# A sliding-window attention block with an MLP on one core: loads six blocks ahead, q and k turned four blocks ahead, and the start and the decay tables rearranged

## The chip, the core and the metric

The kernel runs on one core of a Trainium2 chip. The metric is the device time of one execution in microseconds (us). A core has a matrix engine (PE; its weight loads are listed as PEld), a vector engine (DVE), an activation engine (ACT), GpSimd (POOL) and SyncE (SP). Each engine works through its own list of instructions in order. In this kernel POOL and SP mostly issue DMA transfers, each from its own queue.

## The reference

Inputs are q, k, v of shape (8 batches, 8 heads, 576 tokens, 64), a norm gain g_ln (512), and weights w_ch1 (512 x 2048) and w_ch2 (2048 x 512), all in f32.

```python
scores = q @ k.T / sqrt(64)                      # per batch and head
rel = pos[:, None] - pos[None, :]
scores = scores - slope[h] * abs(rel)            # slope[h] = 2 ** -(h + 1)
attn = softmax(where((rel >= 0) & (rel < 128), scores, -1e9))
x = (attn @ v), heads side by side               # (8, 576, 512)
xn = (x - mean(x)) / sqrt(var(x) + 1e-6) * g_ln
out = x + maximum(xn @ w_ch1, 0) @ w_ch2
```

## The kernel before

**Blocks.** The eight batches are taken as four pairs. A pair has nine blocks of 128 tokens: blocks 0 to 7 alternate between its two batches (four each), and block 8 holds the last 64 tokens of both. So there are 36 blocks, numbered n = 0 to 35 in the list order; n = 9p + blk. One load or turn of q or k serves two blocks (one per batch).

**A block's way.** POOL loads q, k (L225, L228) and v (L238) with casts to f16 into raw buffers. q and k are then turned (transposed), so that the head dimension lies on partitions. PE makes the scores (scores, L446; products L423) for the block's own and the preceding 128 tokens. ACT takes the exponential (L432). DVE multiplies with a mask (masks, L443) that holds the window and the decay exp(-slope x distance). PE multiplies with v (L478), DVE divides by the row sums (L486, L487) to give x, and centres or normalizes it (xc, L517 or L553). xc is turned to xT, and the block is then ready for the MLP. On most blocks POOL computes rstd (L534, L537) ahead of xc.

**Two ways of turning.** For the blocks of the first pair, PE turns q, k and xc and ACT or DVE copies them out of PSUM (L295, L324, L325, L574, L575). From the second pair on (`by_dma`), SP turns them with DMA transpositions: q of the one batch, q of the other, k of the one, k of the other (L313), and xT (L529). These wait on SP's queue in list order, and so do the stores of the output (L926, L930).

**The MLP.** Blocks are grouped: six groups of two, then six of four. mlp1 multiplies xT with w1 in units of four products (L734); ACT or DVE applies the relu into ht (L750, L742). Four PSUM buffers (ps_mm) take the units in turn. mlp2 multiplies with w2 (L767); from group 6 on, `fast_mlp2` (L804, L833) does that with seven instead of eight block products. DVE adds x (L851), and SP stores.

**Decay tables.** The masks are exp(-slope x distance), made by `decay` (L118) on ACT, one instruction a head, from the constant `dist` (128 x 896, f16): m_full, used by the first pair; m_ends and m_tail, for the last block of a pair; m_late, for all later pairs.

**What sets the order.** The order is written out by hand: `steps` is a list of steps, each a list of calls. `weave_at(units, places)` hands out the MLP's units and runs a step at each given place, so that every engine's list follows from the order of calls. Up to block 7 the steps are written one by one. From block 8 on a loop makes them: for each n, the value products of n, the scores of n + 2, the statistics and xc of n with the loads for a later block (`load_step`, L629, which issues all of `place` up to it), the masks, and the turns (`turn_at`, L681). Loads run `AHEAD` = 8 blocks ahead. In the loop the turns of q and k by DMA are called with n + 1 and take block n + 5. They read what the loads brought, and the scores of their block read them.

These lines of before stand in the loop:

```python
stats_step = [(stats, n)] + load_step(n)
turns = [turn_at(n + 1)] if n + 1 < count else []
...
steps += [stats_step + to_mask, [(normal, n)], *turns]
```

Of the kernel before, what the change touches and what calls it, by code (L numbers as in the profile page):

```python
# [17 lines left out]
P = 128  # L18
# [12 lines left out]
AHEAD = 8  # L31
# [28 lines left out]
def kernel(  # L60
# [39 lines left out]
    iden_dram = nc.inline_tensor(np.eye(P, dtype=np.float16), name="iden16")  # L100
    dist_dram = nc.inline_tensor(distances(), name="distances")
    dist = consts.tile([P, 7 * P], FP16)
    nc.sync.dma_start(out=dist, in_=dist_dram.ap())
    iden = consts.tile([P, P], FP16)
    ps_sc = [
        ps_scores.tile([P, 2, 4 * P], FP32, name=f"ps_sc{i}", tag=f"ps_sc{i}")
# [8 lines left out]
    m_full = hsum[0]  # L115
    m_tail = consts.tile([P, H, P], FP16)

    def decay(m, at):  # L118

        n = m.shape[2]  # L120
        for h in range(H):
            nc.scalar.activation(  # L122
                out=m[:, h, :],
                in_=dist[:, at * P : at * P + n],
                func=AF.Exp,
                scale=-(2.0 ** (-8.0 * (h + 1) / H)),
            )
# [50 lines left out]
    def combine_w2():  # L178


        for dst, a, b in (
# [5 lines left out]
            for part in range(2):  # L187
# [3 lines left out]
                )  # L191
                yield

    def load_w2(c):
        n = NFB // 4
        nc.gpsimd.dma_start(
            out=w2[:, c * n : (c + 1) * n, :], in_=w2r[:, c * n : (c + 1) * n, :]
        )
# [44 lines left out]

    order = [(p, blk) for p in range(NPAIR) for blk in range(NSLOT)]
    w1s, w2s = ([(f, c) for c in range(4)] for f in (load_w1, load_w2))
    weights = {3: w1s + w2s[:2], 5: w2s[2:]}
    loads, place = [], []
    for n, (p, blk) in enumerate(order):
        for src, tag in ((q, "q"), (k, "k")):
# [22 lines left out]
    def warm(n):  # L272

        if n:
            ps = ps_mm.tile([P, 4 * P], FP32, tag="mm", name="ps_warm")
        for _ in range(n):
            nc.tensor.matmul(ps, ones[:, 0:P], ones, start=True, stop=True)  # L277
# [113 lines left out]
    def attend(p, blk, keys, mask, tag, hps):  # L391

        heads = slice(2 * hps[0], 2 * hps[-1] + 2)
        nk = len(keys)
        if hps[0] == 0:
            home_pool = own_pool if tag == "own" else probs_pool  # L400
            pr = home_pool.tile([P, H, nk, P], FP16, tag=tag, name=tag)
            for t, o in enumerate(keys):
                weights_of.setdefault((p, blk), []).append((pr, t, o))
        else:
            pr = weights_of[p, blk][-1][0]
        at = len(scored) % 2
        banks = ps_sc[at]
        scored.append((p, blk))
        ps = banks.rearrange("p j (n t q) -> p j n t q", n=len(hps), t=nk)
        qt, b = turned["q", p, blk // 2], blk % 2  # L410
        for n, hp in enumerate(hps):
            for t, o in enumerate(keys):
                kt = turned["k", p, o // 2][:, o % 2]
                for j in range(2):
                    rows = slice(j * HALF, (j + 1) * HALF)
                    for c, queries in seen(p, blk, o, t, junk[at] and j == 0):
                        cols = slice(c * HALF, (c + 1) * HALF)
                        at_q, of_q = ps[cols, j, n, t, :], qt[rows, b, hp]
                        if len(of_q.shape) == 3:
                            at_q = at_q.rearrange("p (r c) -> p r c", r=2)  # L420
                        else:
                            at_q, of_q = at_q[:, queries], of_q[:, queries]
                        nc.tensor.matmul(  # L423
                            at_q,
                            kt[rows, hp, cols],
                            of_q,
                            start=True,
                            stop=True,
                        )
        junk[at] = False  # L430
        dst = pr[:, heads].rearrange("p h t q -> p h (t q)")
        nc.scalar.activation(  # L432
            out=dst.rearrange("p (n j) q -> p j n q", j=2),
            in_=ps.rearrange("p j n t q -> p j n (t q)"),
            func=AF.Exp,
            scale=inv_sqrt_d,
        )
        unmasked.setdefault((p, blk), []).append((dst, mask[:, heads, :]))
# [4 lines left out]
            nc.vector.tensor_tensor(out=dst, in0=dst, in1=mask, op=ALU.mult)  # L443
        del todo[:n]

    def scores(p, blk, between=0):  # L446
        low, high, every = [0, 1], [2, 3], [0, 1, 2, 3]
        m = m_late if by_dma(p, blk // 2) else m_full
        if blk == T:
            attend(p, T, [6, 7], m_ends, "probs", low)  # L450
            attend(p, T, [6, 7], m_ends, "probs", high)
        elif blk < 2:
            attend(p, blk, [blk], m[:, :, P:], "own", every)
        else:
            attend(p, blk, [blk - 2, blk], m, "probs", low)
            warm(between)
            attend(p, blk, [blk - 2, blk], m, "probs", high)

    def scores_tail(p):
        attend(p, T, [T], m_tail, "own", [0, 1, 2, 3])  # L460
# [164 lines left out]
        return [(scores,) + order[n]]  # L625

    def load_step(n):
        return [(load_until, place[min(n + AHEAD, count - 1)])]

    def values_steps(n):  # L630
        p, blk = order[n]
# [5 lines left out]
    def x_step(n, copy=nc.vector.tensor_copy):  # L637
        return [(turn_x,) + home[n] + order[n] + (copy,)] if n < BY_DMA else []
# [5 lines left out]
    def masks_of(n, *halves):  # L644
        return [(masks,) + order[n] + halves]
# [8 lines left out]
    steps += warm_step(2) + [turn_step(2, True, (nc.scalar.copy, nc.scalar.copy))]  # L654
    steps += values_steps(1) + warm_step(4)
    steps += [x_step(0, nc.scalar.copy)] + warm_step(2) + [scores_step(2)]
    steps += [masks_of(2, 1) + x_step(1) + [(warm, 2), (scores, 0, 3, 2)]]
    steps += [values_steps(2)[0]]
    steps += [masks_of(2)]
    first = len(steps)  # L660

    steps += [values_steps(2)[1] + masks_of(3)]
    steps += [x_step(2, nc.scalar.copy), *values_steps(3), x_step(3, nc.scalar.copy)]

    steps += [variance_of(0) + variance_of(1), variance_of(2) + variance_of(3)]
    steps += [[(gain_w1, 0, 13)]]

    steps += [turn_step(4, True) + [(gain_w1, 13, 3)], scores_step(4), masks_of(4) + values_steps(4)[0]]
    steps += [values_steps(4)[1], scores_step(5) + [(decay, m_ends, 2)]]
    steps += [x_step(4) + masks_of(5)]  # L670
    steps += [values_steps(5)[0], turn_step(6, True), values_steps(5)[1], scores_step(6)]
    steps += [x_step(5) + masks_of(6), scores_step(7) + variance_of(4), values_steps(6)[0]]

    steps += [values_steps(6)[1], x_step(6) + masks_of(7), variance_of(5) + [(decay, m_late, 5)]]
    steps += [*values_steps(7), x_step(7) + variance_of(6)]
    steps[-1] += turn_step(9)
    steps += [turn_step(8) + variance_of(7), scores_step(8) + turn_step(11)]
    steps += [[(scores_tail, 0)] + scores_step(9) + masks_of(8)]


    def turn_at(n):  # L681
        ahead = [m for m in (n + 3, n + 4) if m < count and order[m][1] % 2 == 0]
        return [
            f
            for m in ahead
            if by_dma(order[m][0], order[m][1] // 2) == (m == n + 4)
            for f in turn_step(m, True)
        ]

    steps.append([])  # L690
    for n in range(8, count):
        first_half, second_half = values_steps(n)
        step = first_half + second_half[:1]
        if n == BY_DMA + 2:
            step = [(turn_x,) + home[n - 1] + order[n - 1] + (nc.scalar.copy,)] + step
        if n + 1 < count and order[n + 1][1] == T:
            step += [(scores_tail, order[n][0])]
        if n + 2 < count:
            step += scores_step(n + 2)
        steps.append(step)  # L700
        to_mask = [m for t in (n + 1, n + 2) if t < count for m in masks_of(t)]
        stats_step = [(stats, n)] + load_step(n)
        turns = [turn_at(n + 1)] if n + 1 < count else []
        if n == HURRIED:
            steps += [[(normal, n - 1)], stats_step + to_mask, [(normal, n)], *turns]
        elif n >= SETTLED:
            steps += [stats_step + to_mask, [(normal, n)], *turns]
        else:
            steps += [stats_step + to_mask, *turns]
            if n != HURRIED - 1:  # L710
                steps.append([(normal, n)])
# [234 lines left out]
    nc.vector.memset(powers[:, 0:1], EPS)  # L946
    nc.vector.memset(powers[:, 1:2], -0.5)
    decay(m_full, 0)
    decay(m_tail, 4)
    load_until(place[3])  # L950
    engine = mybir.EngineType
    with tc.manual_schedule(engines={engine.PE, engine.SP, engine.Pool}):
        with tc.manual_schedule(engines={engine.Activation, engine.DVE}):
            advance_to(first)
            weave_at(mlp1(0, (0, 1)), 2, 7, 8, 9, 13)
            weave_at(mlp1(1), 2, 8, 12)
            weave_at(mlp2(0, ((0, 8), (8, 12), (12, NFB))), 0, 1, 3, 4, 4, 5)
            weave_at(mlp2(1), 0, 1, 2, 3, 4, 6, 6)
            weave_at(mlp1(2), 0, 3, 3, 6, 8, 11)
            weave_at(mlp2(2), 0, 2, 4, 6, 7)  # L960


            weave_at(mlp1(3, (9, 10, 11)), 8, 8, 12, 15)
            weave_at(mlp2(3), 0, 1, 1, 3, 4, 4, 6, 6)
            weave_at(mlp1(4), 0, 4, 8, 10, 10, 14, also=(2, 12))
            weave_at(mlp2(4), 0, 2, 2, 5, 5, 7, also=(1,))
            weave_at(mlp1(5), 0, 4, 4, 6, 8, 10, also=(3, 7, 11))
            weave_at(mlp2(5), 0, 1, 2, 4, 6, 7)
            ring += [ps_mm.tile([P, DM], FP32, tag="mm", name="ps_r") for _ in range(4)]
            for g in range(6, len(GROUPS)):  # L970
                weave_at(
                    mlp1(g), 0, 2, 5, 7, 8, 10, 13, 15, also=(1, 4) if g == 6 else ()
                )
                weave_at(fast_mlp2(g), 1, 3, 6, 7, 7, 10, 12, 13)
# [31 lines left out]
```

## Time and profile before

| | us |
|---|---|
| median of 3 runs | 309.25 (307.91 to 310.70) |
| the profiled execution | 309.62 |
| its span, first to last instruction | 307.8 |
| PE busy | 298.4 |
| DVE busy | 218.8 |
| ACT busy | 171.6 |
| POOL busy | 143.4 |

The profile is one execution; the span is 1.8 us shorter than that execution's own time, since something lies around the instructions. A row of instructions reads: line, engine, operation, output <- inputs, shape; then times. A wait is printed as "engine line <- what released it: us in total, times, longest us". In the chain that ended last, each row has its start, its duration and what it was. Transfers: issuing queue, operation, count, KB each, median us from issue to landing; a transposition shows no KB. The granted clock of PE was 0.992 of full speed as a mean over the span.

### The profile page before, as it was taken

To read this page: it belongs to the slowest core of one execution; us is meant where nothing else is said; L and a number is where in the kernel's file an instruction comes from. 1 tells how busy PE (TensorE), PEld (TensorE's weight loads), DVE (VectorE), ACT (ScalarE), POOL (GpSimd) and SP (SyncE) were. 2 spreads that over 40 slices of the span, in tenths; PEclk is the share of its full clock that TensorE was granted. 3 is DMA by queue.
4 is the path that set the end of the run, shared out by engine and by line. 5 is a ranking of instruction groups with operands and counts; after the bars stand their busy time and mean duration, and the time that the engine had idled before them with its cause. 6 is when DMAs were issued, how large, how long until landed. Compare 5 with 4: busy or idle time off the path is not lost.

```text
span 307.8 us, 8790 instructions
## 1 busy us (share of the span) xinstructions
PE 298.4 (97%) x3627; PEld 200.6 (65%) x3627; DVE 218.8 (71%) x529; ACT 171.6 (56%) x302; POOL 143.4 (47%) x190
## 2 busy tenths in 40 slices
PE   8899999989999999999999999999999999999994
PEld 2458855665858667545875587568656865784583
DVE  2488977857697786757994799479948984761363
ACT  7388766765757656378247724772486257305600
POOL 8843659745379678537575556517310231000001
PEclk9799999999999999999999999999999999999999
DMA  9999999999999999999899999996862050021004
GB/s 112 140 205 205 185 175 135 181 162 156 164 129 140 172 178 126 182 166 146 54 148 230 143 107 138 153 181 63 145 122 53 19 154 19 18 84 71 2 0 136
DMA packets 158026, 39.25 MB, mean 128 GB/s; under 512 B 148993, under 2 KB 153601, under 8 KB 157986
## 3 DMA queue, kind: packets, MB, share of 16 engines
q0 software_dynamic: 107584, 18.49, 88.6%
q1 hardware_dynamic: 50178, 19.88, 40.1%
q8 instruction: 28, 0.46, 0.7%
q10 hardware_dynamic: 224, 0.33, 0.3%
q14 instruction: 12, 0.10, 0.1%
HBM read 36.97 MB, written 9.44 MB: 151 GB/s over the span
## 4 chain that ended last, share of the span: by engine, by line
PE 88%; ACT 4%; DVE 2%; DMA 2%; POOL 1%; issue 1%; DVEq 0%; POOLq 0%
PE ps_r L734 27%; PE ps_r L833 24%; PE ps_m L767 12%; PE ps_m L734 11%; PE ps_sc L423 5%; PE ps_r L478 3%; PE ps_pv L478 3%; ACT probs L432 2%; DMA k<-in_k_dram 2%; PE ps_warm L277 2%; ACT m L122 1%; PE ps_sc L295 1%; DVE o L851 1%; PE ps_tx L574 1%; POOL q L228 1%
## 5 line engine op out<-in xcount | busy, mean ns | idle before, releaser
L734 PEld LDWEIGHTS <-w1g 128*128 128x128 f16 x640 | 61.1, 98 | 49.5 <-issue 2.7
L734 PE MATMUL ps_r<-xT,w1g 128*128 128x512 f16 x384 | 84.8, 379 | 0.0
L432 ACT ACTIVATE probs<-ps_sc 128x1024 f16<-128x1024 f32 x56 | 54.2, 1026 | 53.6 <-PE ps_sc L423 53.6
L750 ACT ACTIVATE ht<-ps_r 128x512 f16<-128x512 f32 x96 | 56.1, 600 | 32.0 <-PE ps_r L734 31.8
L534 POOL TENSOR_TENSOR rstd<-moments,powers 128x1 f32<-128x1 f32 x28 | 14.3, 510 | 99.4 <-DVE moments L580 99.3
L767 PE MATMUL ps_m<-w,ht 128*128 128x512 f16 x192 | 45.3, 380 | 0.0
L833 PE MATMUL ps_r<-w,ht 128*128 128x256 f16 x384 | 43.9, 273 | 0.0
L833 PEld LDWEIGHTS <-ht 128*128 128x128 f16 x384 | 37.2, 98 | 4.7
L238 POOL DMA_DIRECT2D vx<-in_v_dram x40 | 34.8, 877 | 6.1 <-DVE xc L553 2.7
L750 ACT ACTIVATE ht<-ps_m 128x256 f16<-128x256 f32 x91 | 33.0, 389 | 6.4 <-PE ps_m L734 3.5
L734 PE MATMUL ps_m<-xT,w1g 128*128 128x256 f16 x256 | 30.3, 273 | 2.0 <-ACT ht L750 2.0
L767 PEld LDWEIGHTS <-ht 128*128 128x128 f16 x192 | 17.3, 98 | 18.2
L225 POOL DMA_DIRECT2D q<-in_q_dram x30 | 25.6, 858 | 5.4 <-DMA q<-q 4.2
L443 DVE TENSOR_TENSOR probs<-probs,m 128x1024 f16<-128x1024 f16 x44 | 27.7, 672 | 0.0
L225 POOL DMA_DIRECT2D k<-in_k_dram x30 | 25.9, 871 | 2.5 <-DMA k<-k 1.1
L579 DVE BATCH_NORM_STATS2 st<-x 128x6 f32<-128x512 f16 x36 | 24.8, 688 | 0.7
L537 POOL TENSOR_TENSOR rstd<-rstd,powers 128x1 f32<-128x1 f32 x28 | 23.4, 835 | 2.2
L486 DVE RECIPROCAL rec<-ps_r 128x4 f32<-128x4 f32 x36 | 6.3, 175 | 22.7 <-PE ps_r L478 22.7
L833 PE MATMUL ps_r<-w,hs 128*128 128x256 f16 x192 | 21.9, 273 | 0.0
L478 PEld LDWEIGHTS <-probs 128*128 128x128 f16 x448 | 18.7, 97 | 4.6 <-DVE probs L443 0.3
L423 PE MATMUL ps_sc<-q,k 64*64 64x128 f16 (+1 forms) x1088 | 20.2, 210 | 0.5 <-DVE k L325 0.2
L851 DVE TENSOR_TENSOR o<-ps_r,o 128x512 f32<-128x512 f32 (+1 forms) x25 | 16.6, 665 | 5.6 <-PE ps_r L833 5.3
(85 smaller groups left out, 360.4 us busy)
## 6 DMA issues: line engine op xcount, KB each, us to landing
out_dram<-o SPq DMA_DIRECT2D x22, 256.0 KB, 4.3
q<-in_q_dram POOLq DMA_DIRECT2D x32, 128.0 KB, 8.4
k<-in_k_dram POOLq DMA_DIRECT2D x32, 128.0 KB, 8.2
vx<-in_v_dram POOLq DMA_DIRECT2D x32, 128.0 KB, 9.3
w<-in_moe_w_ch_dram POOLq DMA_DIRECT2D x8, 512.0 KB, 10.4
out_dram<-o SPq DMA_DIRECT2D x24, 128.0 KB, 5.4
q<-in_q_dram POOLq DMA_DIRECT2D x8, 64.0 KB, 5.1
k<-in_k_dram POOLq DMA_DIRECT2D x8, 64.0 KB, 5.5
```

The costliest lines, as they stand in the source:

```text
L225: nc.gpsimd.dma_start(out=dst, in_=rows.rearrange("h p d -> p h d"))
L238: nc.gpsimd.dma_start(out=vx[p0 : p0 + n, :, 0:D], in_=v[b, :, t0 : t0 + n, :].rearrange("h p d -> p h d"),)
L423: nc.tensor.matmul(at_q, kt[rows, hp, cols], of_q, start=True, stop=True,)
L432: nc.scalar.activation(out=dst.rearrange("p (n j) q -> p j n q", j=2), in_=ps.rearrange("p j n t q -> p j n (t q)"), func=AF.Exp, scale=in ...
L443: nc.vector.tensor_tensor(out=dst, in0=dst, in1=mask, op=ALU.mult)
L478: nc.tensor.matmul(ps[:, i, :], pr[:, h, t, :], vext[(p * NSLOT + o) % NV][:, h, :], start=(n == 0), stop=(n == len(terms) - 1),)
L537: nc.gpsimd.tensor_tensor(out=here, in0=here, in1=powers[:, 1:2], op=ALU.pow)
L579: nc.vector.bn_stats(out=st, in_=xs[order[n]])
L734: nc.tensor.matmul(ps[:, 0:cols], w[:, kb, fb * P : (fb + 1) * P], xT[:, kb, 0:cols], start=(kb == 0), stop=(kb == NKB - 1),)
L750: nc.scalar.activation(out=ht[:, fb, 0:cols], in_=ps[:, 0:cols], func=AF.Relu)
L767: nc.tensor.matmul(sums[at], ht[:, fb, at * P : (at + 1) * P], w2[:, fb, :], start=(fb == 0), stop=(fb == NFB - 1),)
L833: nc.tensor.matmul(banks[name][pair][:, pair, :], lhs[:, fb, pair * P : (pair + 1) * P], rhs[:, fb, :], start=(first and fb == 0 and (pair ...
```

## The change

- The first transfer of dist brings 256 of its 896 columns; POOL brings the others after the last w2 loads, ahead of the loads for block 6.
- The m_tail table is no longer made at the start. m_ends, m_tail and m_late are now made in pieces of two, four and two heads, one piece a step over the last ten steps but two of the list written by hand. On ACT they come out as: exponentials of block 6, 2 of m_ends, exponentials of block 7, 4 of m_ends, a relu of group 2, 2 of m_ends, three relus, 8 of m_tail, three relus, and m_late in twos between the following relus, the last two after a copy of k.
- In the start, two warm-up products go; the scores of block 3 are made in two halves, with two units of mlp1 between them; mlp1 of group 0 begins two units earlier on PE; on DVE the xT copy of block 1 precedes a mask, and the masks of block 3 precede the centring of block 2.
- Loads: steps 9 and 10 issue none, and from then on step n issues the loads for block n + 6.
- In the loop, the DMA turns of q and k are called with n and take block n + 4; they come behind the xT transposition of block n on SP, and one step later than before.

```diff
--- before.py
+++ after.py
@@ -100,7 +100,7 @@
     iden_dram = nc.inline_tensor(np.eye(P, dtype=np.float16), name="iden16")
     dist_dram = nc.inline_tensor(distances(), name="distances")
     dist = consts.tile([P, 7 * P], FP16)
-    nc.sync.dma_start(out=dist, in_=dist_dram.ap())
+    nc.sync.dma_start(out=dist[:, 0 : 2 * P], in_=dist_dram.ap()[:, 0 : 2 * P])
     iden = consts.tile([P, P], FP16)
     ps_sc = [
         ps_scores.tile([P, 2, 4 * P], FP32, name=f"ps_sc{i}", tag=f"ps_sc{i}")
@@ -115,10 +115,10 @@
     m_full = hsum[0]
     m_tail = consts.tile([P, H, P], FP16)
 
-    def decay(m, at):
+    def decay(m, at, heads=range(H)):
 
         n = m.shape[2]
-        for h in range(H):
+        for h in heads:
             nc.scalar.activation(
                 out=m[:, h, :],
                 in_=dist[:, at * P : at * P + n],
@@ -191,6 +191,9 @@
                 )
                 yield
 
+    def load_distances():
+        nc.gpsimd.dma_start(out=dist[:, 2 * P :], in_=dist_dram.ap()[:, 2 * P :])
+
     def load_w2(c):
         n = NFB // 4
         nc.gpsimd.dma_start(
@@ -243,7 +246,7 @@
 
     order = [(p, blk) for p in range(NPAIR) for blk in range(NSLOT)]
     w1s, w2s = ([(f, c) for c in range(4)] for f in (load_w1, load_w2))
-    weights = {3: w1s + w2s[:2], 5: w2s[2:]}
+    weights = {3: w1s + w2s[:2], 5: w2s[2:] + [(load_distances,)]}
     loads, place = [], []
     for n, (p, blk) in enumerate(order):
         for src, tag in ((q, "q"), (k, "k")):
@@ -443,7 +446,7 @@
             nc.vector.tensor_tensor(out=dst, in0=dst, in1=mask, op=ALU.mult)
         del todo[:n]
 
-    def scores(p, blk, between=0):
+    def scores(p, blk, halves=(0, 1)):
         low, high, every = [0, 1], [2, 3], [0, 1, 2, 3]
         m = m_late if by_dma(p, blk // 2) else m_full
         if blk == T:
@@ -452,9 +455,8 @@
         elif blk < 2:
             attend(p, blk, [blk], m[:, :, P:], "own", every)
         else:
-            attend(p, blk, [blk - 2, blk], m, "probs", low)
-            warm(between)
-            attend(p, blk, [blk - 2, blk], m, "probs", high)
+            for half in halves:
+                attend(p, blk, [blk - 2, blk], m, "probs", (low, high)[half])
 
     def scores_tail(p):
         attend(p, T, [T], m_tail, "own", [0, 1, 2, 3])
@@ -625,7 +627,8 @@
         return [(scores,) + order[n]]
 
     def load_step(n):
-        return [(load_until, place[min(n + AHEAD, count - 1)])]
+        ahead = AHEAD - min(max(n - BY_DMA, 0), 2)
+        return [(load_until, place[min(n + ahead, count - 1)])]
 
     def values_steps(n):
         p, blk = order[n]
@@ -654,38 +657,41 @@
     steps += warm_step(2) + [turn_step(2, True, (nc.scalar.copy, nc.scalar.copy))]
     steps += values_steps(1) + warm_step(4)
     steps += [x_step(0, nc.scalar.copy)] + warm_step(2) + [scores_step(2)]
-    steps += [masks_of(2, 1) + x_step(1) + [(warm, 2), (scores, 0, 3, 2)]]
-    steps += [values_steps(2)[0]]
-    steps += [masks_of(2)]
+    steps += [x_step(1) + [(warm, 2), (scores, 0, 3, (0,))] + masks_of(2, 1)]
     first = len(steps)
 
-    steps += [values_steps(2)[1] + masks_of(3)]
-    steps += [x_step(2, nc.scalar.copy), *values_steps(3), x_step(3, nc.scalar.copy)]
+    products, centring = zip(*((h[0], h[1]) for h in map(values_steps, (2, 3))))
+    steps += [masks_of(2), [(scores, 0, 3, (1,))], products[0]]
+    steps += [centring[0][:1] + masks_of(3) + centring[0][1:], products[1]]
+    steps += [centring[1], x_step(2, nc.scalar.copy), x_step(3, nc.scalar.copy)]
 
     steps += [variance_of(0) + variance_of(1), variance_of(2) + variance_of(3)]
     steps += [[(gain_w1, 0, 13)]]
 
     steps += [turn_step(4, True) + [(gain_w1, 13, 3)], scores_step(4), masks_of(4) + values_steps(4)[0]]
-    steps += [values_steps(4)[1], scores_step(5) + [(decay, m_ends, 2)]]
+    steps += [values_steps(4)[1], scores_step(5)]
     steps += [x_step(4) + masks_of(5)]
     steps += [values_steps(5)[0], turn_step(6, True), values_steps(5)[1], scores_step(6)]
     steps += [x_step(5) + masks_of(6), scores_step(7) + variance_of(4), values_steps(6)[0]]
 
-    steps += [values_steps(6)[1], x_step(6) + masks_of(7), variance_of(5) + [(decay, m_late, 5)]]
+    steps += [values_steps(6)[1], x_step(6) + masks_of(7), variance_of(5)]
     steps += [*values_steps(7), x_step(7) + variance_of(6)]
     steps[-1] += turn_step(9)
     steps += [turn_step(8) + variance_of(7), scores_step(8) + turn_step(11)]
     steps += [[(scores_tail, 0)] + scores_step(9) + masks_of(8)]
 
 
+    tables = [
+        (decay, m, at, range(h, h + n))
+        for m, at, n in ((m_ends, 2, 2), (m_tail, 4, 4), (m_late, 5, 2))
+        for h in range(0, H, n)
+    ]
+    for step, table in zip(steps[-len(tables) - 2 :], tables):
+        step.append(table)
+
     def turn_at(n):
-        ahead = [m for m in (n + 3, n + 4) if m < count and order[m][1] % 2 == 0]
-        return [
-            f
-            for m in ahead
-            if by_dma(order[m][0], order[m][1] // 2) == (m == n + 4)
-            for f in turn_step(m, True)
-        ]
+        m = n + 4
+        return turn_step(m) if m < count and order[m][1] % 2 == 0 else []
 
     steps.append([])
     for n in range(8, count):
@@ -700,7 +706,7 @@
         steps.append(step)
         to_mask = [m for t in (n + 1, n + 2) if t < count for m in masks_of(t)]
         stats_step = [(stats, n)] + load_step(n)
-        turns = [turn_at(n + 1)] if n + 1 < count else []
+        turns = [turn_at(n)]
         if n == HURRIED:
             steps += [[(normal, n - 1)], stats_step + to_mask, [(normal, n)], *turns]
         elif n >= SETTLED:
@@ -946,13 +952,12 @@
     nc.vector.memset(powers[:, 0:1], EPS)
     nc.vector.memset(powers[:, 1:2], -0.5)
     decay(m_full, 0)
-    decay(m_tail, 4)
     load_until(place[3])
     engine = mybir.EngineType
     with tc.manual_schedule(engines={engine.PE, engine.SP, engine.Pool}):
         with tc.manual_schedule(engines={engine.Activation, engine.DVE}):
             advance_to(first)
-            weave_at(mlp1(0, (0, 1)), 2, 7, 8, 9, 13)
+            weave_at(mlp1(0, (0, 1)), 0, 1, 2, 3, 6, 7, 8, 12)
             weave_at(mlp1(1), 2, 8, 12)
             weave_at(mlp2(0, ((0, 8), (8, 12), (12, NFB))), 0, 1, 3, 4, 4, 5)
             weave_at(mlp2(1), 0, 1, 2, 3, 4, 6, 6)
```

## The prediction

> **What bounds the kernel now.** I read the page's busy table first, then the waits of PE, the chain that ended last, and for every place where the change moves something the timeline of that engine.
>
> ```profile
> PE 298.4 (97%) x3627; PEld 200.6 (65%) x3627; DVE 218.8 (71%) x529; ACT 171.6 (56%) x302; POOL 143.4 (47%) x190
> DMA  9999999999999999999899999996862050021004
> PE ps_m L734 <- ACT ht L750: 2.0, 4, 1.1
> ```
>
> PE is busy 97% of the span, and its largest wait on another engine after the start is 2.0 us in four pieces, for relu outputs of ACT. From about 130 us to the end PE has no gap. PE does the same work after the change (two 512-column warm-up products fewer), so there is little to win, and the question is where PE is made to wait. The DMA row says that transfers fill the first two thirds; they are now early enough that PE waits for none after 21 us.
>
> ```profile
> 27.10 1.75 PE ps_m L734 x16
> 28.88 0.40 PE ps_tx L574 x4
> 29.28 7.86 PE ps_m L734 x72
> ...
> 59.14 0.38 ACT ht L750
> 59.52 2.44 ACT m L122 x8
> 61.96 0.28 ACT ht L750
> 62.28 1.03 PE ps_m L734 x8
> ```
>
> These are two stretches of the chain (start, us, what). At 28.88 PE turns block 3, the last that the first MLP group still lacked; 18 units of four products (72) are then left, at 7.86/18 = 0.436 us. At 59.52 eight decays of m_late hold ACT for 2.44 us between two relus, and PE, out of PSUM buffers, stands 1.28 us until 62.28.
>
> **The front: 0 (-0.5 to +0.4).** It drops eight m_tail decays (8 x 0.211 = 1.69 us of ACT) ahead of the first k copy, and a dist transfer of 224 KB becomes 64 KB. ACT finished those decays before k's landing let PE begin at 9.47, so the landing is the limit. The smaller transfer could bring it forward by at most 0.3 us: the first packets of q come 0.9 us after its issue here, 0.64 us in the quiet at 211 us. DVE sets the rest:
>
> ```profile
> 20.08 0.69 DVE L443 TENSOR_TENSOR probs<-probs,hs 128x1024 f16<-128x1024 f16 x1 [0.99 <-ACT probs L432]
> ```
>
> From 20.08 on DVE is nearly full up to the centring of block 3. The xT copy (0.42 us) that moves into the 0.99 us idle ahead of that mask brings block 3's turn from 28.88 to about 28.47. But of the 32 units of this group 19, not 18, are then left (76 products in the new order). PE reaches "18 left" at 28.47 + 0.23 + 0.436 = 29.14, against 29.11 before: nothing. The split of block 3's scores moves PE work of the same size only, and the two dropped warm-up products (0.43 us together) lie in PE's spare time ahead of DVE. The bounds are the two DVE gaps of 0.2 us that might also go, and one unit of 0.436.
>
> **The decays: +1.0 (-1.3 to +1.5).** Before, ACT makes the m_ends tables around 45 us, in idle time. Now they, m_tail and m_late are strewn between the exponentials of blocks 6 and 7 and the relus of the third MLP group. From 55.8 us on ACT then has 5.34 us of decays (4 m_ends and 8 m_late at 0.305, 8 m_tail at 0.211) where it had 2.44. I replayed 55.8 to 68 us by hand with the durations of this trace: exponential 0.96, relu 0.37, unit of PE 0.436, value product 0.25, four PSUM buffers. The replay gives the old stall's end at 62.28, and with the new order: unit 3 waits until 59.3 (58.5 before), unit 7 until 63.1 because all eight m_tail decays (60.96 to 62.65) stand in front of one relu, and the next group starts at 67.9 instead of 66.9. What hides a decay elsewhere is four buffers, about 4 x 0.436 = 1.7 us of PE's work; eight m_tail in a row are just that. If the spreading worked, the old 1.28 would go.
>
> The other 160 KB of dist cost POOL one issue (0.75 us, as its w2 loads) ahead of the loads for block 6, which landed at 42.9 to 45.5 for a turn on PE at 49.1; its first reader comes after 50 us: 0.
>
> **Loads six ahead: 0 by itself.** POOL skips two steps and later issues the same transfers two blocks later. Loads took 8 to 12 us between 78 and 140 us and six blocks are over 30 us; the cover is ample. One DVE wait on POOL goes:
>
> ```profile
> 98.31 0.41 DVE L517 TENSOR_SCALAR xc<-x,moments,rstd 128x512 f16<-128x512 f16 x1 [0.73 <-POOL rstd L537]
> ```
>
> rstd of block 11 no longer stands behind loads, so this xc ends at 97.98 instead of 98.72.
>
> **q and k turned four ahead: +5.4 (0 to 14.5).** The four transpositions of a pair (q, q, k, k) move one step back on SP's queue and now stand behind the xT transposition of block n, which waits for xc of block n. The scores need the first and the third. SP's pace:
>
> ```profile
> 93.88 2.53 SPq L313 DMA_TRANSPOSE k<-k x2
> ...
> 219.56 2.53 SPq L313 DMA_TRANSPOSE q<-q x2
> 222.20 2.50 SPq L313 DMA_TRANSPOSE k<-k x2
> ```
>
> One holds SP 1.25 us and the next begins 1.3 us after it. So k's first begins 0.03 + 1.3 (xT) + 2 x 1.3 = about 3.97 us after xc. From issue to landing, by the DMA view of four stretches (90:97, 172:179, 202:209, 219:236 us; last column the median us):
>
> ```profile
> q<-q SPq DMA_TRANSPOSE x2, 6.5
> k<-k SPq DMA_TRANSPOSE x2, 6.9
> ...
> q<-q SPq DMA_TRANSPOSE x2, 7.5
> k<-k SPq DMA_TRANSPOSE x2, 5.6
> ...
> q<-q SPq DMA_TRANSPOSE x2, 3.2
> k<-k SPq DMA_TRANSPOSE x2, 4.7
> ...
> q<-q SPq DMA_TRANSPOSE x3, 2.4
> k<-k SPq DMA_TRANSPOSE x3, 2.4
> ```
>
> With loads in flight 5 to 7 us, alone 2.4. Against that stand PE's deadlines, the first score product of the block:
>
> ```profile
> 105.70 0.54 PE L423 MATMUL ps_sc<-q,k 64*64 64x128 f16 x32
> 189.18 0.54 PE L423 MATMUL ps_sc<-q,k 64*64 64x64 f16 x32
> ```
>
> (Blocks 15 and 27.) Each sum is xc + 3.98, plus landing, against the deadline:
> Block 15, behind xc of 11: 97.98 + 3.98 = 101.96, + 5.8 (the second q of 92.55) = 107.76, deadline 105.70: +2.1 (0 to 3.5).
> Block 20, behind xc of 16 (126.88): 130.86 + 6.5 = 137.4, deadline 136.95: +0.4 (0 to 3.0 with the 9.1 that its k took).
> Block 24, behind xc of 20 (157.24): 161.2 + 5.8 = 167.0, deadline 167.0: 0 (0 to 1.7 with 7.5).
> Block 27, behind xc of 23 (182.17): 186.15 + 5.2 (the second k of 176.40) = 191.35, deadline 189.18: +2.1 (0 to 4.5).
> Block 31, behind xc of 27 (212.29): 216.27 + 3.7 (the first q of 202.38) = 220.0, deadline 219.2: +0.8 (0 to 1.8).
> Blocks 13, 17, 18, 22, 26, 29, 33 and 35 have 2 us and more to spare. A stall shifts xc and deadlines behind it alike, so the terms add. I took the lower rows of each place since fewer loads are queued. Before, these landed 3 to 11 us ahead of use; that was their cover. What PE does not get done while it waits is only postponed: ACT and DVE, behind it, wait with it.
>
> The xT transpositions gain what q and k lose (block 13's waited from 109.8 to 116.7 behind a set), but no PE wait is for them, so they return nothing.
>
> A rule on this: the Trainium skill, "DMA: Bandwidth & Descriptors", section "Issuing engines are not separate DMA queues", says that transfers started by different engines run on the same 16 DMA engines and interleave. By it SP's transpositions stay slow while POOL loads, and the term stays 5.4; were SP's path its own, each would land in 2.4 and the term be 0. The trace agrees with the rule (6.9 among loads, 2.4 without). Section "Queues, rings and completion order" of the same page adds that an engine takes turns between queue rows packet by packet, by which a shorter row of loads would not help as long as any load is pending; no run here shows that yet.
>
> **Sum.** The profiled execution took 309.6 us, 307.8 of it span. 309.6 + 0 + 1.0 + 0 + 5.4 = 316.0; it lies 0.4 above the median of the runs, so 315.6.
>
> **Rivals.** (a) The turns land in time: with two blocks fewer in flight a landing under 3.7 us at block 15 and under 2.9 to 3.1 at 27 and 31 is enough. With 2.4 all four meet their deadlines and only the decays are left: 309.2 + 1.0 = 310.2. For it: POOL's queue is shorter. Against: the same three loads a block are issued just ahead of the set. (b) The other side: as (a), and the decays in twos fit under four buffers, so that the stall ended at 62.28 goes: 309.2 - 1.3 - 0.5 (front) = 307.4. It decides if a relu never stands behind more than 1.7 us of other ACT work. Against it: m_tail in one piece. (c) The landings keep the slower row of each place: 6.9 at block 15 (+3.2), 8.4 at 20 (+2.3), 6.5 at 24 (+0.7), 5.6 at 27 (+2.5), 4.7 at 31 (+1.8): 10.5, thus 320.7.
>
> **Chances.** Forecast 0.55, with a range of its own of 312 to 318; (a) 0.20; (b) 0.12; (c) 0.13. Faster and slower count from 1% (306.2 and 312.3 us), about what a measurement of this kernel can tell. Faster 0.07, about half of (b) with more of the front; within 1% 0.28, from the rest of (b), nearly all of (a) and the forecast's low end; slower 0.65. The range, 308.5 to 319.8, leaves out some of (b) and the upper half of (c).
>
> **What would show it.** PE waits on "DMA k<-k" ahead of the scores of blocks 15, 27 and 31, of 1 to 3 us each, and none of them at 17, 18 or 33; SP's set behind xT; ACT's relu wait near 62 us grown by 1 us; the turn of block 3 at 28.5. If PE shows no wait for k from 95 us on, the largest term is wrong, and with it the forecast; if the stall at 62 us is gone, the replay is.

## The result, and the profile after

The changed kernel takes 325.13 us (median of 5 runs, 323.23 to 328.46), the kernel before 308.72 (5 runs in the same comparison): a ratio of 1.0507, 95% interval 1.0474 to 1.0540. The change makes the kernel 5% slower. The forecast had the sign and the main mechanism, but 315.6 us, and the time lies above its range. One of the five runs (328.46 us) and one of the twelve with one late set below (315.16) are over 1.5% slower than the fastest of their kernel; the medians and ranges given here include them, the ratios do not. The profiled execution spans 323.3 us, 15.5 more than before.

The busy row, the clock row (tenths of full speed in 40 slices) and the row of DMA engines of the changed kernel:

```profile
PE 302.0 (93%) x3625; PEld 201.8 (62%) x3625; DVE 218.4 (68%) x529; ACT 171.2 (53%) x302; POOL 142.7 (44%) x191
PEclk9999999999999998999999997999989999999998
DMA  9999999999949999999799989994994073003004
```

No engine has more to do. PE's share falls from 97% to 93%, its busy time rises by 3.6 us although it runs two products fewer, and the clock row, flat before except at its start, has three dips (the 8 in the last slice is the end of the kernel, after PE's last product). So PE waits more, and some of its products run slower. What it waits for, in the view of waits of PE (line numbers shift by 3 to 6; L426 is the score product, L740 mlp1, L756 the relu):

```profile
PE ps_sc L426 <- DMA k<-k: 8.0, 5, 2.8
PE ps_sc L426 <- DMA q<-q: 2.6, 3, 1.6
PE ps_m L740 <- ACT ht L756: 2.5, 6, 0.7
```

Before, there was no wait for a turned q or k at all; now there are 10.6 us of them. The timeline of PE shows the largest, at the scores of blocks 18, 27 and 31 (start, duration, then in brackets the idle time before the row and what ended it):

```profile
126.80 0.46 PE L426 MATMUL ps_sc<-q,k 64*64 64x128 f16 x16 [2.00 <-DMA k<-k]
127.19 5.00 PE L773 MATMUL ps_m<-w,ht 128*128 128x512 f16 x15
...
199.23 0.64 PE L426 MATMUL ps_sc<-q,k 64*64 64x128 f16 x16 [2.79 <-DMA k<-k]
...
232.11 0.25 PE L426 MATMUL ps_sc<-q,k 64*64 64x128 f16 x4 [1.62 <-DMA q<-q]
233.46 0.80 PE L426 MATMUL ps_sc<-q,k 64*64 64x128 f16 x28 [1.11 <-DMA k<-k]
```

In the second row 15 products of 512 columns take 5.0 us, a third of a microsecond each instead of about 0.216 (the same products have starts 0.216 us apart at 56.3 to 56.9 us in the profile before). The view by windows (start:end, length, busy time and instructions of each engine, then the granted clock) shows why:

```profile
123.63:127.04 3.41, 1.41 (x51) 1.07 (x48) 2.56 (x7) 1.02 (x1) 0.47 (x1) 1.00 2.28 145
127.04:130.45 3.41, 3.41 (x21) 1.17 (x11) 0.71 (x2) 1.02 (x1) 3.27 (x5) 0.50 1.84 166
130.45:133.87 3.42, 3.42 (x17) 1.56 (x16) 1.01 (x2) 0.00 (x0) 0.00 (x0) 1.00 1.70 174
195.31:198.72 3.41, 1.13 (x36) 0.93 (x34) 3.17 (x9) 1.02 (x1) 1.53 (x3) 1.00 1.74 167
198.72:202.13 3.41, 2.90 (x22) 1.29 (x23) 1.35 (x3) 1.43 (x2) 3.33 (x5) 0.50 1.82 219
229.44:232.85 3.41, 1.29 (x26) 0.99 (x23) 3.17 (x9) 0.00 (x0) 0.00 (x0) 1.00 1.93 163
232.85:236.27 3.42, 2.81 (x33) 1.35 (x34) 1.08 (x3) 2.09 (x3) 3.16 (x6) 0.50 1.15 348
```

After each of these three waits PE is granted half its clock (0.50) for 3.41 us. Half of PE's busy time in those windows is an estimate of what that costs: 1.71 + 1.45 + 1.40 = 4.6 us. Together with the waits (10.55 us by the rows of the timeline) this is 15.1 us.

### The profile page after: what moved, and what is told of

The parts are those of the page before. It is cut to its first block, busy times and chain, and to the rows that moved or that the text cites. A ratio compares the mean times of both kernels' runs of the same rounds, so it can differ in the third digit from the quotient of the medians.

```text
span 323.3 us, 8785 instructions
## 1 busy us (share of the span) xinstructions
PE 302.0 (93%) x3625; PEld 201.8 (62%) x3625; DVE 218.4 (68%) x529; ACT 171.2 (53%) x302; POOL 142.7 (44%) x191
## 4 chain that ended last, share of the span: by engine, by line
PE 72%; DMA 14%; DVE 4%; POOL 4%; ACT 4%; issue 1%; SPq 1%; DVEq 0%; ACTq 0%; POOLq 0%
PE ps_r L740 24%; PE ps_r L839 21%; PE ps_m L773 11%; DMA k<-k 9%; PE ps_m L740 7%; DMA w<-in_moe_w_ch_dram 4%; PE ps_sc L426 4%; PE ps_r L480 2%; ACT probs L435 2%; PE ps_pv L480 1%; POOL vx L241 1%; DVE x L489 1%; POOL q L231 1%; ACT ht L756 1%; SPq L316 1%
## 5 line engine op out<-in xcount | busy, mean ns | idle before, releaser
L740 PEld LDWEIGHTS <-w1g 128*128 128x128 f16 x640 | 61.7, 99 | 51.8 <-issue 6.3
L740 PE MATMUL ps_r<-xT,w1g 128*128 128x512 f16 x384 | 86.9, 386 | 0.0
L756 ACT ACTIVATE ht<-ps_r 128x512 f16<-128x512 f32 x96 | 56.4, 599 | 34.5 <-PE ps_r L740 34.2
L536 POOL TENSOR_TENSOR rstd<-moments,powers 128x1 f32<-128x1 f32 x28 | 13.3, 477 | 113.1 <-DVE moments L582 113.0
L773 PE MATMUL ps_m<-w,ht 128*128 128x512 f16 x192 | 46.9, 390 | 0.0
L241 POOL DMA_DIRECT2D vx<-in_v_dram x40 | 35.0, 883 | 10.5 <-PE ps_m L740 4.8
L756 ACT ACTIVATE ht<-ps_m 128x256 f16<-128x256 f32 x91 | 32.5, 394 | 6.3 <-PE ps_m L740 4.0
L740 PE MATMUL ps_m<-xT,w1g 128*128 128x256 f16 x256 | 30.4, 273 | 2.3 <-ACT ht L756 2.2
L426 PE MATMUL ps_sc<-q,k 64*64 64x128 f16 (+1 forms) x1088 | 21.3, 211 | 11.1 <-DMA k<-k 8.0
L426 PEld LDWEIGHTS <-k 64*64 64x64 f16 x1088 | 15.5, 109 | 17.0 <-DMA k<-k 8.6
L488 DVE RECIPROCAL rec<-ps_r 128x4 f32<-128x4 f32 x36 | 6.3, 175 | 28.5 <-PE ps_r L480 28.5
L539 POOL TENSOR_TENSOR rstd<-rstd,powers 128x1 f32<-128x1 f32 x28 | 22.1, 790 | 2.2
L435 ACT ACTIVATE own<-ps_sc 128x1024 f16<-128x1024 f32 x12 | 12.1, 1022 | 20.6 <-PE ps_sc L426 20.1
```

What stands on the lines that cost most here:

```text
L241: nc.gpsimd.dma_start(out=vx[p0 : p0 + n, :, 0:D], in_=v[b, :, t0 : t0 + n, :].rearrange("h p d -> p h d"),)
L426: nc.tensor.matmul(at_q, kt[rows, hp, cols], of_q, start=True, stop=True,)
L435: nc.scalar.activation(out=dst.rearrange("p (n j) q -> p j n q", j=2), in_=ps.rearrange("p j n t q -> p j n (t q)"), func=AF.Exp, scale=in ...
L536: nc.gpsimd.tensor_tensor(out=here, in0=moments[:, n, 1:2], in1=powers[:, 0:1], op=ALU.add)
L539: nc.gpsimd.tensor_tensor(out=here, in0=here, in1=powers[:, 1:2], op=ALU.pow)
L740: nc.tensor.matmul(ps[:, 0:cols], w[:, kb, fb * P : (fb + 1) * P], xT[:, kb, 0:cols], start=(kb == 0), stop=(kb == NKB - 1),)
```

## The experiments

All ratios are against the kernel before, run on the same chip at the same time. Not all experiments ran on one chip, so small differences between their medians are less certain than those between the ratios.

**The turns back to five ahead, all else changed.**

```diff
-        turns = [turn_at(n)]
+        turns = [turn_at(n + 1)] if n + 1 < count else []
```

> The changed kernel with one thing undone: the turns of q and k go back to five blocks ahead; loads stay six ahead, the start and the decay tables stay changed. Theory (the turns behind xT of the block four before are what PE waits for, and the half-clock windows follow from these waits): PE waits for no turn after 30 us, no half-clock window between 30 and 300 us, and the time falls by 15 to 17 us to 307 to 310 us. Rival 1 (fewer loads ahead is what hurts): it stays above 318. Rival 2 (half and half: the turn of the changed kernel is late because the loads that moved two blocks now run beside it): 311 to 316, with some waits for k left.

Measured: 308.28 us (307.37 to 309.43), ratio 0.9976 (0.9951 to 1.0000). PE waits for no turn, and its clock is 1.00 from 4.7 to 305 us. This one line takes away 16.9 us of 325.13 by the medians, 16.4 by the ratios. The whole loss, half-clock windows included, hangs on the turns. This kernel has the same start and tables as the changed one, and its profiled span is 306.8 us, 16.5 less: the 15.1 us counted above are most of that, and 1.4 stay unassigned.

**Only the turns four ahead, on the kernel before.**

```diff
-        turns = [turn_at(n + 1)] if n + 1 < count else []
+        turns = [turn_at(n)]
```

> The kernel before with one thing done: q and k turned four blocks ahead; loads stay eight ahead, start and tables as before. Theory (lateness on SP's queue is enough): waits for turns of about 8 to 12 us at blocks 15, 17, 18, 24 and 27, at least one half-clock window after a wait of over 2 us, 318 to 326 us. At block 31 the loads of the last blocks are over by then, so its wait of 3.1 us in the changed kernel should shrink to under 1 us. Rival (the loads six ahead are needed for it): within 1% of 308.7.

Measured: 328.90 us (326.63 to 329.93), ratio 1.0643 (1.0580 to 1.0706); PE's waits:

```profile
PE ps_sc L423 <- DMA k<-k: 8.2, 4, 2.9
PE ps_sc L423 <- DMA q<-q: 3.8, 3, 2.0
```

The lateness alone is enough. It is even dearer than the whole change: 12.0 us of waits against 10.6, and 17.1 us at half clock (two windows of 6.8 us and one of 3.4) against 10.2. So loads six ahead may lessen the damage of late turns; but the start and the tables differ too, and how many windows halve changes from run to run (mean clocks 0.967 to 0.983 here, 0.979 to 0.993 in the changed kernel), so their share isn't shown. One part of the expectation failed: at block 31 PE stood 1.08 + 1.15 = 2.2 us, not under 1 (in the changed kernel it stood 2.7, not 3.1). The DMA view of that stretch, 226 to 235 us, shows what ran beside the set:

```profile
q<-in_q_dram POOLq DMA_DIRECT2D x2, 64.0 KB, 3.0
k<-in_k_dram POOLq DMA_DIRECT2D x2, 64.0 KB, 5.2
vx<-in_v_dram POOLq DMA_DIRECT2D x2, 64.0 KB, 6.5
q<-q SPq DMA_TRANSPOSE x2, 6.6
```

With loads eight ahead these six are the loads of the last block. POOL issues them right after rstd of block 27, just before the xc that releases the set. So the set lands in 6.6 us here too, for a different reason than in the changed kernel, where the loads two blocks earlier run beside it.

**Only the loads six ahead, on the kernel before.**

```diff
-        return [(load_until, place[min(n + AHEAD, count - 1)])]
+        ahead = AHEAD - min(max(n - BY_DMA, 0), 2)
+        return [(load_until, place[min(n + ahead, count - 1)])]
```

> The kernel before with one thing done: loads six blocks ahead from block 10 on. Theory (six blocks are over 30 us, the cover is ample, and turns five ahead still land in time): 308 to 310 us, no wait of PE for a transfer after 30 us. Rival (the loads now run beside the turns that used to find a quiet queue, landing grows from 3 to 7 us): 310 to 314 with waits for k near blocks 27 to 31.

Measured: 308.20 us (307.58 to 311.51), ratio 0.9998 (0.9966 to 1.0030), no wait of PE for a turn. The loads cost nothing while the turns are early.

**Only the start and the tables** (both distances undone):

> The changed kernel with both distances undone (turns five ahead, loads eight ahead): only the changed start and the decay tables are left. Theory (the start gains about 1.0 us, the tables cost about 0.5 us): 308.0 to 309, that is 0.997 to 1.001 of before. Rival (the tables cost the whole 1.0 us of the prediction and the start gains nothing): 309.5 to 310.5.

Measured: 308.34 us (307.47 to 309.28), ratio 0.9977 (0.9950 to 1.0004). This is the theory's number, but the interval just reaches no change. It is hardly the gain that the theory meant, though. One window of 3.41 us at half clock makes the mean clock of a run 0.994 (1 - 1.7/308). Of the kernel before, 15 of 25 runs had 0.994 or less (median 309.42 us) and 10 had 0.997 or more (308.54); the ten runs here, and the ten with turns five ahead, all had 0.997 or more. Among runs without such a window the gain is 0.2 us; the section on the prediction comes back to it, under the front.

**The turns four ahead, but before the statistics of the block.**

```diff
-        stats_step = [(stats, n)] + load_step(n)
-        turns = [turn_at(n)]
+        stats_step = turn_at(n) + [(stats, n)] + load_step(n)
+        turns = [[]]
```

> The changed kernel with the turns of q and k still called at n for block n + 4, but ahead of the statistics of block n, so that they stand before and not behind xT of block n on SP; the calls up to n = 14 already had them before xT of their own n, except n = 11. Theory (place behind xc is what makes a set late): blocks 15, 24, 27 and 31 get their k 4 us and more before the scores; blocks 17 and 18, whose sets stand behind output stores that wait for the MLP, keep waits of together 2 to 4 us; 310 to 314 us. Rival (four blocks are too few wherever the set stands, since what is ahead on SP holds it): waits remain at 24, 27 and 31, 318 us or more.

Measured: 309.33 us (308.62 to 311.61), ratio 1.0014 (0.9980 to 1.0049). Of all waits for turns one of 0.3 us is left:

```profile
PE ps_sc L426 <- DMA k<-k: 0.3, 1, 0.3
```

So "four blocks ahead" is not what costs, or only about 1 us of it: the ratio lies 0.004 above that of the turns five ahead (0.9976), though both profiled executions took 308.62 us. What costs is the place on SP, for most sets behind xc of block n. Blocks 17 and 18, where I had expected 2 to 4 us of waits, are in time too: called ahead of the statistics, the set for 17 also stands ahead of the output stores that held it. SP's timeline in the changed kernel, and then in this one:

```profile
110.40 1.11 SPq L932 DMA_DIRECT2D out_dram<-o  x2
111.63 1.78 SPq L316 DMA_TRANSPOSE q<-q  x1
114.02 1.20 SPq L316 DMA_TRANSPOSE k<-k  x1
115.32 1.21 SPq L531 DMA_TRANSPOSE xT<-xc  x1
116.62 0.54 SPq L932 DMA_DIRECT2D out_dram<-o  x1
117.27 2.69 SPq L316 DMA_TRANSPOSE q<-q  x2
120.06 2.99 SPq L316 DMA_TRANSPOSE k<-k  x2
```

```profile
103.65 1.21 SPq L316 DMA_TRANSPOSE q<-q  x1
105.05 1.29 SPq L316 DMA_TRANSPOSE k<-k  x1
108.03 1.11 SPq L932 DMA_DIRECT2D out_dram<-o  x2
109.25 1.47 SPq L531 DMA_TRANSPOSE xT<-xc  x1
110.81 0.61 SPq L932 DMA_DIRECT2D out_dram<-o  x1
111.53 2.73 SPq L316 DMA_TRANSPOSE q<-q  x2
114.36 3.32 SPq L316 DMA_TRANSPOSE k<-k  x2
```

In the first the pair of block 17 (one q, one k) begins at 111.63, behind two stores; that pushes xT and the set of block 18 back to 117.27. In the second the pair begins at 103.65 and the set of 18 at 111.53.

**Spare products where PE waited**, in `attend`, 9, 13 and 14 for blocks 18, 27 and 31:

```diff
+        for _ in range({(2, 0): 9, (3, 0): 13, (3, 4): 14}.get((p, blk), 0) * (hps[0] == 0)):
+            nc.tensor.matmul(banks[:, 0, :], iden, ones, start=True, stop=True)
```

> The changed kernel with spare products on PE (128x128 by 128x512 of constants into the score bank, overwritten by the scores) ahead of the scores of blocks 18, 27 and 31: 9, 13 and 14 of them, 1.9, 2.8 and 3.0 us, as long as PE waited there. Nothing arrives earlier. Theory (PE's idle time itself brings the half-clock windows behind it): the waits for k and q at these three blocks shrink to under 0.5 us each, no half-clock window is left between 30 and 300 us, and the time falls by the 3.9 us that those windows cost, to 320 to 322 us. Rival (the half clock comes from elsewhere, and idle time has no part in it): windows stay, 325 us or, if the products lie on the path, more.

Measured: 322.90 us (322.11 to 325.35), ratio 1.0447 (1.0372 to 1.0521); in the profiled run the clock is 1.00 from 7.2 to 321 us. The half clock goes when PE is kept busy, with all transfers issued as they were; of the three other runs two still have mean clocks of 0.995 and 0.992. The time lies above what was expected, and the interval overlaps that of the changed kernel: at block 18 a wait of 1.7 us remained, since k landed at 128.3 there (126.8 in the changed kernel).

**One late set alone**: five ahead everywhere, block 27 four ahead, first without and then with 13 spare products.

```diff
-        turns = [turn_at(n)]
+        turns = [turn_at(n if n == 23 else n + 1)] if n != 22 and n + 1 < count else [[]]
```

> The changed kernel with all turns five ahead but the one set for block 27, which stays four ahead. Against the kernel with all five ahead (308.3 us): k of block 27 begins at xc of block 23 + 4 us = 185.2 and lands 6 us later, at 191.2, for scores at 188.2. Theory: PE waits 3.0 us there, a half-clock window of 3.4 us follows and costs 1.3 to 1.7 us, 312.3 to 313.0. Rival 1 (only the wait counts): 311.3. Rival 2 (PE catches up by later slack): under 310.

> The same with 13 spare products (2.8 us, constants into the score bank, overwritten) on PE ahead of the scores of block 27. Theory (idle time brings the half clock): PE waits 0.2 to 0.5 us, no half-clock window behind it, 311.1 to 311.6, so 1.2 to 1.5 us faster than the same kernel without them although PE does more. Rival (the half clock has another cause): the same time as without them, or slower.

Measured: 311.13 us (309.46 to 315.16), ratio 1.0064 (1.0028 to 1.0101), without; 311.15 us (310.57 to 312.12), ratio 1.0058 (1.0029 to 1.0087), with them. The windows around the late set, without the products:

```profile
186.05:189.47 3.42, 1.40 (x39) 1.18 (x36) 3.18 (x10) 1.02 (x1) 1.65 (x2) 1.00 1.78 162
189.47:192.88 3.41, 2.01 (x20) 0.98 (x21) 0.87 (x3) 1.02 (x1) 3.21 (x5) 0.50 1.76 237
192.88:196.29 3.41, 3.41 (x10) 1.22 (x8) 0.76 (x2) 1.20 (x2) 0.54 (x1) 0.50 1.69 149
```

With them no window is at half clock, and the profiled span is 310.3 us against 311.9. But the medians are equal, so the expected 1.2 to 1.5 us did not come: 2.8 us of products and a remaining wait of 0.9 add up to more than the wait of 3.4 us that they replaced. By these numbers the rivals are right: 311.3 for the wait alone, and the same time with the products. What does differ is the spread, 4.3 us (309.46 to 313.72, without the run at 315.16) against 1.6. One late set costs 2.9 us at the median (311.13 against 308.28), not the 4.0 to 4.7 expected.

The mean clock of each run shows what the medians hide. Without the products seven of the twelve runs have 0.999 or more (median 310.3 us), three have 0.994 to 0.995, as with one window at half clock (312.25 to 312.81), and two 0.989, as with two (313.72, which is the profiled one, and 315.16). With the products all twelve have 0.997 or more. So at the median the products cost 0.8 us against the runs that lost no clock, and save 1.1 us or more against each of the others.

The windows of all twelve profiles together, from 30 to 299 us, say when the clock halves. Seven windows of 3.41 us in which PE was busy 0.69 to 1.41 us were followed by half clock. Ten with 1.70 to 2.35 us were not. Two of these ten are one wait of 2.58 us, at block 27 of the kernel with only the turns changed, that a window's edge cut in two:

```profile
199.63:203.05 3.42, 2.34 (x47) 2.02 (x45) 3.25 (x9) 1.02 (x1) 2.59 (x3) 1.00 1.72 172
203.05:206.46 3.41, 1.91 (x24) 1.00 (x25) 1.85 (x5) 1.44 (x3) 2.29 (x4) 1.00 1.94 195
```

So the same wait costs more or less by where the windows' edges fall, which are elsewhere in each profile. That the edges decide which runs of the kernel with one late set lose the clock is likely, but only one of its runs has a profile.

**The tables where ACT is idle**, with turns five ahead, and then on the kernel before with nothing else changed:

```diff
-    steps += [values_steps(4)[1], scores_step(5)]
+    steps += [values_steps(4)[1], scores_step(5) + [(decay, m_ends, 2), (decay, m_late, 5, range(4))]]
...
-    steps += [values_steps(5)[0], turn_step(6, True), values_steps(5)[1], scores_step(6)]
+    steps += [values_steps(5)[0], turn_step(6, True), values_steps(5)[1], scores_step(6) + [(decay, m_tail, 4)]]
...
+    steps[-3].append((decay, m_late, 5, range(4, H)))
```

The list of pieces (`tables`) is dropped in the first. The second leaves m_tail where it was, so that the middle pair of lines is not in it, and drops the one call that made all of m_late.

> The changed kernel with turns five ahead, and the decay tables put where ACT stood idle: all of m_ends and half of m_late after the exponentials of block 5, m_tail after those of block 6, the other half of m_late after the k copy ahead of block 9. Theory (PE's relu waits between 57 and 64 us, 1.9 us with turns five ahead, come from decays standing among the relus): the waits at 57, 58 and 60 us go, about 1.6 us less than with turns five ahead alone, 306.4 to 307.2 us, faster than before by 0.6 to 0.9%. Rival (the relus are late for their own reasons, PE merely waits elsewhere): 308.0 to 308.5.

> The kernel before with only the tables moved: m_tail stays at the start, m_ends and half of m_late after the exponentials of block 5, the other half of m_late after the k copy ahead of block 9. Theory: the stall of 1.28 us near 61 us goes, most of the 0.28 beside it stays since it waits for DVE, 307.5 to 308.1 us. Rival: within 0.2 us of before.

Measured: 306.97 us (306.52 to 308.06), ratio 0.9930 (0.9907 to 0.9953), with the changed start; 307.51 us (306.94 to 308.99), ratio 0.9950 (0.9928 to 0.9971), on the kernel before. Both are clear of no change. PE's wait for relus falls from 2.5 us to 1.2 in the first:

```profile
PE ps_m L734 <- ACT ht L750: 1.2, 4, 0.3
```

In the second it falls from 2.0 to 0.9. The first of the two is the fastest version here: 0.7% faster than before, 5.6% faster than the changed kernel. Part of this is again the clock at the start: of the 23 runs of the kernel before beside them, the nine with a mean clock of 0.997 or more have a median of 308.14 us; the twelve of the first kernel, all at 0.997 or more, lie 1.2 us below that, and the eight such runs of the second (307.22) 0.9, near the 1.1 us by which its relu waits fell.

## Why the prediction was wrong

**The step that failed is the term of the turns.** Its mechanism is right: undone, the loss is gone; alone, it makes the whole loss. Its size was 5.4 us where it came to 15.1, for three reasons. By block, the wait forecast and PE's idle time in the profile after:

| block | forecast | idle | first k (31: first q): forecast landing time, then measured |
|---|---|---|---|
| 15 | 2.1 | 1.2 | 5.8, 4.6 |
| 17 | 0 | 0.65 | - |
| 18 | 0 | 2.0 | -, 6.7 |
| 20 | 0.4 | 0 | 6.5, 2.4 |
| 24 | 0 | 1.2 | 5.8, 6.4 |
| 27 | 2.1 | 2.8 | 5.2, 6.0 |
| 31 | 0.8 | 2.7 | 3.7, 7.2 |

First, the half clock was left out, 4.6 us. The prediction counted a wait at its own length. The runs show that a wait that leaves PE busy for only 0.69 to 1.41 of a window's 3.41 us also halves the clock of the next one. The Trainium skill, "TensorE: Matmul & The Clock Gate", Part 1, describes a free-running window of 3413 ns and warns of PE gaps longer than about that. The windows here have that length, but gaps of 2.0 us inside one were enough; the measurement decides.

Second, blocks 17 and 18 were called safe, and cost 2.65 us. The prediction's sum for a set counts the xT transposition ahead of it on SP and nothing else. For these two it is not even xT of block n, as the list of the change has it, that stands ahead: with n = 13 and 14 the loop calls the turns before xc, and xT of block 13 at 115.32 follows the pair for 17. What holds that pair are the two output stores at 110.40, and what holds the set for 18 are that pair, xT of block 13 and a third store. Everything that the step is moved behind had to be counted, on the queue itself.

Third, block 31 was sized by the wrong row. The 3.7 us were the landing of its first q at 202.38, where the set used to run and the last load beside it landed at 205.50. The set moved to 224.89, among loads issued from 222.43 on; there its q took 7.2 us. A landing has to be read where the transfer goes, not where it comes from. At blocks 15 and 20 the rows were too slow, at 24 and 27 too fast; these four together came to 5.2 us where 4.6 were forecast, which is partly luck. (A slip without effect: 0.03 + 1.3 + 2 x 1.3 is 3.93, where the sums have 3.98.)

**The rivals.** (a) asked for landings under 3.7 us with fewer loads in flight; only block 20 had one (2.4). Whether fewer loads helped at all isn't shown; they did not help enough. (b) is out with it; its half about the tables is answered below. (c), 320.7 us, was nearest; it too lacked the half clock. That its 10.5 us of waits equal the 10.55 measured is luck: 2.3 of them are at block 20, which had none, and none at 17 and 18.

**Loads six ahead: 0** was right: 0.9998 (0.9966 to 1.0030) alone.

**The decays: +1.0** had the sign and twice the size. The relu waits and turn waits of PE between 57 and 65 us, start to start, are 0.77 + 0.23 + 0.86 + 0.41 = 2.3 us after and 0.28 + 1.28 + 0.24 = 1.8 before: +0.5. The m_tail decays in one piece (59.55 to 61.28 on ACT) made the third of them, as the prediction said, but 0.86 us where the old stall had 1.28. That the decays among the relus hold PE there is shown by the two kernels with the tables in ACT's idle time, where these relu waits are gone; what is left is PE's wait for an xc before a turn, 0.57 and 0.30 us.

**The front: 0** was a little short. The first k landed 1.5 us earlier, not at most 0.3; these are rows of the chain, of before and of after:

```profile
3.46 5.97 DMA k<-in_k_dram
```

```profile
12.52 14.48 DMA w<-in_moe_w_ch_dram
27.00 0.05 issue
27.05 0.61 PE ps_m L740 x4
```

Before, PE began when the k issued at 3.46 had landed, at 9.43; after, that k landed at 7.95 and the start is bound by a transfer of w1, which lands at 27.00 (27.13 before). So in this profile most of the gain is caught by the next transfer, and the DVE order by which I had argued 0 is not what bound the start. Where PE takes up the scores of block 4, eight profiles with the new start lie at 37.5 to 39.2 us, mean 38.3; four with the old one at 37.8 to 39.8, mean 39.1. That is 0.7 us, with ranges that overlap.

But three of the four old ones, the profile before among them, lost a window of the clock at the start, and none of the eight new ones did. These are windows of before:

```profile
6.11:9.52 3.41, 2.53 (x43) 0.99 (x46) 0.76 (x2) 1.32 (x7) 3.41 (x5) 1.00 2.58 153
9.52:12.94 3.42, 3.42 (x67) 1.80 (x68) 1.29 (x2) 1.55 (x2) 2.12 (x4) 0.50 2.43 138
```

The one old start without such a window, in the kernel before with only the tables moved, is at 37.8, earlier than the mean of the new ones. The mean clocks of all runs agree: 0.994 or less in 42 of 77 runs of the kernel before and in 7 of 22 of the two other kernels with the old start and early turns, but in one of 54 of the five kernels with the new start in which PE waits for no turn longer than 0.9 us. So what the new start gains is mainly that window, a term that the prediction did not have; what in the start prevents it, the earlier k or another step, was not tested.

**The signs named beforehand** came as written for the waits at 15, 27 and 31 and for SP's set behind xT. "None at 17 or 18" was the sign that the term was wrong, and so it was. Two others did not come: no relu wait near 62 us grew by 1 us, the one there is 0.86 us, and block 3 was turned at 27.49 us, not at 28.5. So the replay of ACT and the sum for the front were off in their parts too, by less.

## What to carry to other kernels

Before a transfer is issued later, list all that then stands ahead of it on its own queue, and what each of those waits for: here xc, stores and another set together used up slack that looked like 3 to 11 us. "How many blocks ahead" says little; with the same four blocks ahead, but placed before the wait for xc, the kernel loses about 1 us instead of 16. And price a wait of PE with the clock that it may lose behind it.

## What the runs showed of the hardware beyond expectation

PE's granted clock changed, in each profile, only at edges that lie multiples of 3.41 us apart. From 30 to 299 us, after one with PE busy 1.41 us or less the next ran at 0.50, after 1.70 us or more it did not; at half clock, windows with 2.81 us of busy time and more brought full clock back, and windows with 1.97, 2.01 and 2.57 us did not, so that one wait of 3.4 us cost 6.8 us of half clock. Nothing here was run to place the limits more closely. In the kernel before with only the tables moved, the window that holds PE's last products, 1.45 us of them, was not followed by half clock. At the start of the kernel that limit fails: the first window recorded at full clock had PE busy 2.53, 2.61 and 2.87 us in the three profiles whose next window ran at half, and 3.20 us or more in the nine others.

SP's transposition landed in 2.4 us with no load beside it and in 4.6 to 7.2 us at the blocks that were late.
